# A dynamic convolution with a token-choosing expert layer: softmax sums moved to VectorE in stages, score sums in contiguous reads, x loaded first, a shorter plan for ranks and experts

## The chip, the cores and the metric

The kernel runs on one core of a Trainium2 chip. A core has TensorE (PE, matrix products, weights loaded beforehand), VectorE (DVE), ScalarE (ACT), GpSimd (POOL) and SyncE (SP, which here only issues transfers). Each works through its own queue in order, and semaphores hold an instruction until what it needs is ready. Sixteen DMA engines move data between DRAM and the on-chip memory, SBUF; TensorE writes its products to PSUM, which VectorE and ScalarE read. The metric is the device time of one execution in microseconds.

## The reference, cut to what matters

```python
# x: (8, 4160, 192) float32; weight_gen: (8, 4160, 8 heads, 7 taps)
w = exp(weight_gen - max); w = w / (sum of w over the 7 taps + 1e-9)
conv[b, s, h, :] = sum over k of w[b, s, h, k] * x_pad[b, s + k, h, :]   # 24 channels a head, 6 zeros ahead

scores = einsum('bsd,d->bs', conv, w_gate)
out = conv.copy()
for b in range(8):
    top = indices of the 128 largest scores[b]
    ye = maximum(conv[b, top] @ w1, 0) @ w2        # 192 -> 1024 -> 192
    out[b, top] = conv[b, top] + sigmoid(scores[b, top])[:, None] * ye
```

## The kernel before, in words

**Tiling.** A batch of 4,160 positions is cut into 35 windows of 120; there are 280 windows. x is loaded in fp16 in 20 chunks of 14 windows (`load_x`, L135, issued by GpSimd), a window with its six earlier positions on the 128 partitions; ten chunk buffers exist. The work is in three groups of 2, 3 and 3 batches, that is 70, 105 and 105 windows.

**Softmax of a group.** The windows lie on partitions, the 120 positions in four chunks of 32, 32, 32 and 24 (`WCH`). For each chunk `load_w` (L192) brings the raw weights through SP's queue into one of two buffers. `softmax_a` (L219) takes Exp on ScalarE into the group's buffer `amem` (L227; two such buffers, groups 0 and 2 share one), sums over the seven taps by seven identity matmuls into the PSUM bank `misc` (L235), and takes Ln and Exp(-x) on ScalarE (L241, L243). `softmax_b` (L250) multiplies on VectorE (L257). `wt_head` (L265) transposes one head's weights, eight transposes and a copy; the last one clears a corner on GpSimd (L285).

**Convolution.** A step is four windows; there are 72 steps, and each is also a slot of the plan. `band` (L663) writes, on VectorE, the banded matrices of a step from the transposed weights and a mask; `conv` (L680) runs 32 matmuls of 24 columns with them; `evac` (L723) copies PSUM to SBUF on ScalarE and issues the stores on SP.

**Scores.** The score of a position is the convolution of y = x times the gate per head. `y_unit_a` and `y_unit_b` (L291, L304) transpose x in units of eight blocks, copy on ScalarE and multiply by the gate. For a group whose y is complete, `score_t` (L334) transposes y; `score_p` (L351), once for even and once for odd positions, multiplies weights with shifted y on VectorE and sums over eight heads and seven taps by 56 identity matmuls of 60 columns (L370); `score_s` (L375) copies the sums on ScalarE and sends them to DRAM and back in another layout, issued on SP.

**Selection and experts.** `sel_cand` (L453) takes 24 candidates from each partition, `sel_bcast` (L463) sends them through DRAM to all partitions and prepares values, `sel_rank` (L496) counts ranks on ScalarE and VectorE, `sel_hot` (L510) sorts by one-hot matmuls and `sel_fin` (L527) makes lists and gates. Then per batch `ex_gather` (L598) fetches 128 rows of the result from DRAM, `ex_a`, `ex_h` and `ex_y` (L610, L621, L632) compute the expert, and a scatter writes the rows back.

**Order.** Every engine's queue is written out by hand through a plan: lists of moves per slot. In each slot come `band` of the next step, `conv`, the slot's moves and then `evac` (L896 to L911). Behind step 72 the plan goes on with empty slots that hold only moves.

```python
for si in range(NS):
    if si + 1 < NS:
        band(si + 1)
    conv(si)
    for mv in pre[si] + plan[si]:
        mv()
    evac(si)
```

The softmax of group 1 has a chunk in slots 2, 4, 6 and 8, that of group 2 in slots 27, 29, 31 and 33. The scores begin in slots 13, 33 and 51, candidates are in slot 56, the finished selection in slot 64, and a batch's gather, transposes, hidden layer and output are in slots s, s+2, s+3 and s+4, with s two further for each batch.

## Time and profile before

| | us |
|---|---|
| median of 3 runs | 375.7 |
| lowest and highest | 375.44, 375.74 |
| profiled execution, its own time | 376.66 |
| its span, first to last instruction | 374.9 |

The profile is of one execution. An engine's busy time says how long its instructions ran, not whether anything waited for them; the chain of waits follows the work that ended last back from the end, each step to what released it. Times inside the rows are microseconds from the span's start unless marked ns. PE is a matmul, PEld a weight load, POOLq and SPq an engine's issue of transfers. L with a number is a line of the kernel before. A row of busy time by window has the window, its length, the busy time of PE, PEld, DVE, ACT and POOL with their instructions, the clock granted to TensorE as a share of 2.4 GHz, the busy share of the DMA engines and GB/s.

### The profile page before, as it was taken

To read this page: it belongs to the slowest core of one execution; us is meant where nothing else is said; L and a number is where in the kernel's file an instruction comes from. 1 tells how busy PE (TensorE), PEld (TensorE's weight loads), DVE (VectorE), ACT (ScalarE), POOL (GpSimd) and SP (SyncE) were. 2 spreads that over 40 slices of the span, in tenths; PEclk is the share of its full clock that TensorE was granted. 3 is DMA by queue.
4 is the path that set the end of the run, shared out by engine and by line. 5 is a ranking of instruction groups with operands and counts; after the bars stand their busy time and mean duration, and the time that the engine had idled before them with its cause. 6 is when DMAs were issued, how large, how long until landed. Compare 5 with 4: busy or idle time off the path is not lost.

```text
span 374.9 us, 9170 instructions
## 1 busy us (share of the span) xinstructions
PE 260.0 (69%) x3950; PEld 207.8 (55%) x3950; DVE 205.7 (55%) x197; ACT 181.9 (49%) x300; POOL 59.2 (16%) x110
## 2 busy tenths in 40 slices
PE   0355567778779977477778988887833254999991
PEld 0111465557679867355468977887832143654440
DVE  4322658546743667525455467995499999600000
ACT  1343276656873466556662399763135713332220
POOL 3300393022100111031100100000000003134231
PEclk9999999955885555855655589555555555555555
DMA  8756099999999489989932735464143424340110
GB/s 140 112 107 148 10 197 227 235 214 218 222 210 193 68 178 215 224 230 220 140 81 79 110 75 145 132 172 136 39 131 102 119 75 138 90 123 31 31 33 16
DMA packets 77404, 50.30 MB, mean 134 GB/s; under 512 B 42128, under 2 KB 75792, under 8 KB 77359
## 3 DMA queue, kind: packets, MB, share of 16 engines
q0 software_dynamic: 38256, 16.11, 34.8%
q1 hardware_dynamic: 38655, 33.56, 33.8%
q8 instruction: 32, 0.52, 0.6%
q14 instruction: 13, 0.11, 0.1%
q10 hardware_dynamic: 448, 0.00, 0.1%
HBM read 37.70 MB, written 26.49 MB: 171 GB/s over the span
## 4 chain that ended last, share of the span: by engine, by line
PE 44%; ACT 21%; DVE 15%; DMA 9%; issue 6%; SPq 2%; POOL 1%; ACTq 0%; POOLq 0%; DVEq 0%
PE misc L370 10%; PE misc L235 9%; ACT xT L301 7%; ACT amem L227 5%; DMA out_dram<-co 5%; PE xtps L297 5%; DMA wraw<-in_weight_gen_dram 4%; PE hps L626 4%; PE hps L628 4%; PE cps L704 4%; DVE band__158 L668 3%; PE yeps L636 3%; DVE band__159 L668 3%; ACT co L729 3%; ACT wt L282 2%
## 5 line engine op out<-in xcount | busy, mean ns | idle before, releaser
L668 DVE TENSOR_TENSOR band__158<-wt,mask 128x3840 f16<-128x3840 f16 (+1 forms) x36 | 75.9, 2110 | 21.7 <-PE cps L704 14.9
L668 DVE TENSOR_TENSOR band__159<-wt,mask 128x3840 f16<-128x3840 f16 (+2 forms) x36 | 75.0, 2082 | 10.4 <-PE cps L704 10.3
L729 ACT COPY co<-cps 128x768 f32<-128x768 f32 x70 | 55.9, 802 | 33.3 <-PE cps L704 17.5
L235 PE MATMUL misc<-amem,ident 105*105 105x256 f16 (+3 forms) x84 | 37.7, 602 | 47.4 <-ACT amem L227 47.4
L301 ACT COPY xT<-xtps 128x1024 f16<-128x1024 f16 (+1 forms) x60 | 53.6, 913 | 31.1 <-PE xtps L297 30.4
L235 PEld LDWEIGHTS <-ident 105*105 105x105 f16 (+1 forms) x84 | 14.6, 173 | 65.3 <-issue 59.6
L297 PE MATMUL xtps<-ident,x 128*128 128x128 f16 x420 | 48.5, 291 | 0.0
L704 PE MATMUL cps<-x,band__158 128*128 128x24 f16 x1128 | 36.3, 181 | 16.7 <-DVE band__158 L668 16.4
L704 PEld LDWEIGHTS <-band__158 128*128 128x128 f16 x1128 | 35.9, 105 | 19.9 <-DVE band__158 L668 17.1
L257 DVE TENSOR_TENSOR amem<-amem,r 105x2048 f16<-105x2048 f16 (+3 forms) x12 | 13.9, 1157 | 57.6 <-ACT r L243 57.6
L704 PE MATMUL cps<-x,band__159 128*128 128x24 f16 x1112 | 35.8, 181 | 13.7 <-DVE band__159 L668 10.0
L704 PEld LDWEIGHTS <-band__159 128*128 128x128 f16 x1112 | 35.2, 105 | 17.4 <-DVE band__159 L668 10.5
L370 PE MATMUL misc<-sp,ident 105*105 105x60 f16 (+1 forms) x336 | 37.9, 288 | 5.6 <-DVE sp L360 5.6
L370 PEld LDWEIGHTS <-ident 105*105 105x105 f16 (+1 forms) x336 | 37.4, 177 | 5.7 <-issue 5.7
L297 PEld LDWEIGHTS <-x 128*128 128x128 f16 x420 | 37.6, 132 | 0.0
L156 POOL DMA_DIRECT2D x<-in_x_dram x24 | 25.3, 1073 | 65.6 <-PE cps L704 59.3
L227 ACT ACTIVATE amem<-wraw 105x1792 f16<-105x1792 f32 (+3 forms) x12 | 19.3, 1604 | 13.0 <-DVE rmax L763 10.2
L241 ACT ACTIVATE lnd<-misc 105x256 f32<-105x256 f32 (+3 forms) x12 | 4.4, 368 | 38.7 <-PE misc L235 38.7
L360 DVE TENSOR_TENSOR sp<-amem,Y 105x3840 f16<-105x3840 f16 (+1 forms) x6 | 12.9, 2157 | 17.2 <-PE misc L370 13.5
L274 PE MATMUL wtps<-ident,amem 105*128 105x105 f16 (+1 forms) x192 | 14.8, 235 | 9.3 <-ACT xT L301 5.7
L630 ACT ACTIVATE hT<-hps 128x512 bf16<-128x512 f32 x16 | 9.6, 597 | 23.4 <-PE hps L628 21.8
L626 PE MATMUL hps<-xeT,w_a 128*128 128x128 bf16 x64 | 18.3, 286 | 2.4 <-ACT xeT L616 2.4
(137 smaller groups left out, 302.0 us busy)
## 6 DMA issues: line engine op xcount, KB each, us to landing
out_dram<-co SPq DMA_DIRECT2D x64, 360.0 KB, 4.3
x<-in_x_dram POOLq DMA_DIRECT2D x14, 672.0 KB, 20.2
wraw<-in_weight_gen_dram SPq DMA_DIRECT2D x24, 224.0 KB, 5.8
x<-in_x_dram POOLq DMA_DIRECT2D x8, 336.0 KB, 17.1
wraw<-in_weight_gen_dram SPq DMA_DIRECT2D x8, 168.0 KB, 4.2
x<-in_x_dram POOLq DMA_DIRECT2D x2, 624.0 KB
out_dram<-co SPq DMA_DIRECT2D x5, 180.0 KB, 3.9
out_dram<-co SPq DMA_DIRECT2D x6, 90.0 KB, 3.7
```

Source lines behind the costliest of these rows:

```text
L156: nc.gpsimd.dma_start(out=t[p0:p0 + n, lo - c * CW:hi - c * CW, :], in_=ap_of(x_flat, x_flat.offset + (row0(lo) + off) * D, [[D, n], [W * ...
L227: nc.scalar.activation(out=A[0:n, :, q0:q1, 0:K].rearrange("p c q k -> p q c k"), in_=wr[0:n, 0:nq * M, :].rearrange("p (q m) (h k) -> p q ...
L235: nc.tensor.matmul(out=dv[0:n], lhsT=ident16[0:n, 0:n], rhs=A[0:n, :, q0:q1, k], start=(k == 0), stop=(k == K - 1),)
L274: nc.tensor.transpose(out=tp[:, m, 0:n], in_=am[0:n, o:o + P], identity=ident16[0:n, 0:n])
L297: nc.tensor.transpose(out=tp[:, r - r0, :], in_=xf[:, r * P:(r + 1) * P], identity=ident16[:, :])
L301: nc.scalar.copy(out=xT[:, 0:r1 - r0, :], in_=tp[:, 0:r1 - r0, :])
L370: nc.tensor.matmul(out=sps[0:n, odd], lhsT=ident16[0:n, 0:n], rhs=sp[0:n, :, h, :, k], start=(h == 0 and k == 0), stop=(h == H - 1 and k = ...
L626: nc.tensor.matmul(out=hps[:, t, :], lhsT=w1_a[:, c0:c0 + P], rhs=xeT[:, 0, :], start=True, stop=False)
L628: nc.tensor.matmul(out=hps[:, t, :], lhsT=w1_b[0:64, c0:c0 + P], rhs=xeT[0:64, 1, :], start=False, stop=True)
L668: nc.vector.tensor_tensor(out=bt[:, 0:n * H * BC].rearrange("p (c q m) -> p c q m", q=NQ, m=M), in0=wts[gi][:, l:l + n].rearrange("p w h m ...
L704: nc.tensor.matmul(out=cps[:, w // 2, (w % 2) * D + h * G:(w % 2) * D + (h + 1) * G], lhsT=bt[:, o:o + P], rhs=xwin(g + w)[:, h * G:(h + 1 ...
L729: nc.scalar.copy(out=co[:, 0:n, :].rearrange("p (j w) d -> p j (w d)", w=2), in_=cps[:, 0:n2, 0:2 * D],)
```

## The change: what it does

The branches for a layout that is not used (`HALF`) are gone; this changes no instruction. The rest:

- **Softmax in four stages.** `sm_exp` (ScalarE), `sm_den` (a VectorE sum over the seven taps, in place of the seven matmuls), `sm_r` (Ln and Exp) and `sm_norm` (the multiplication) stand in four slots one after another. Group 1 has a chunk in each of slots 0 to 3, group 2 in slots 23, 25, 27 and 29. Heads are transposed one a slot instead of two.
- **Score sums.** Eight identity matmuls of 480 contiguous columns sum over heads (`score_m`), a slot after the product, and a VectorE sum over the taps reads PSUM; the copy on ScalarE goes. The transfers of scores and of candidates are issued on GpSimd.
- **Start.** Ten x chunks are issued at the start, eight of them before the softmax of group 0 instead of behind it. Only the unused eighth tap of `amem` is cleared, for the first buffer on VectorE, for the second on GpSimd. The four chunks of group 0 are interleaved by stage. The selection's constants move from slot 2 to the start.
- **Order in a slot.** `band` runs two steps ahead with three buffers, `evac` comes right behind `conv`. A unit of y is multiplied behind the next unit's transposes; the last one ends in slot 53 instead of 50 and the scores begin in slots 14, 34 and 53.
- **Selection and experts.** Candidates are in slot 58, the finished selection in slot 63; batches follow each other by one slot, with the four parts in s, s+1, s+2 and s+3, and four buffers for gathered rows.
- **PSUM.** The bank `misc` goes, and its bank becomes a third buffer for transposes, sums and expert outputs.

```diff
-    ps_t = ctx.enter_context(tc.tile_pool(name="ps_t", bufs=2, space=bass.MemoryType.PSUM))
+    ps_t = ctx.enter_context(tc.tile_pool(name="ps_t", bufs=3, space=bass.MemoryType.PSUM))
...
-        den = misc[:, 0:M * H * 4]
-        dv = den[:, 0:M * H * nq].rearrange("p (c q) -> p c q", q=nq)
-        for k in range(K):
-            nc.tensor.matmul(
-                out=dv[0:n], lhsT=ident16[0:n, 0:n], rhs=A[0:n, :, q0:q1, k],
-                start=(k == 0), stop=(k == K - 1),
-            )
-        cq = M * H * nq
-        lnd = smp.tile([P, M * H * 4], FP32, tag="lnd", name="lnd")
-        nc.scalar.activation(out=lnd[0:n, 0:cq], in_=den[0:n, 0:cq], func=AF.Ln)
...
+        n, q0, q1, nq, col, cq = dims(gi, ci)
+        den = smp.tile([P, M * H * 4], FP32, tag="den", name="den")
+        nc.vector.tensor_reduce(
+            out=den[0:n, 0:cq].rearrange("p (c q) -> p c q", q=nq),
+            in_=a_view(gi)[0:n, :, q0:q1, 0:K], axis=AX.X, op=ALU.add,
+        )
...
+    def sm_r(gi, ci):
+        n, q0, q1, nq, col, cq = dims(gi, ci)
+        den = sm[(gi, ci)]
+        nc.scalar.activation(out=den[0:n, 0:cq], in_=den[0:n, 0:cq], func=AF.Ln)
         r2 = smp.tile([P, M * H * 4, 2], FP16, tag="r2", name="r2")
...
+    def score_m(gi, odd):
+        b0, b1 = GROUPS[gi]
+        n = (b1 - b0) * NW
+        sp = sps_.pop((gi, odd))
+        sps = ps_t.tile([P, M // 2, Q, 8], FP32, tag="tps", name="sps")
         for h in range(H):
-            for k in range(K):
-                nc.tensor.matmul(
-                    out=sps[0:n, odd], lhsT=ident16[0:n, 0:n], rhs=sp[0:n, :, h, :, k],
-                    start=(h == 0 and k == 0), stop=(h == H - 1 and k == K - 1),
-                )
+            nc.tensor.matmul(
+                out=sps[0:n].rearrange("p m q k -> p m (q k)"), lhsT=ident16[0:n, 0:n],
+                rhs=sp[0:n, :, h, :], start=(h == 0), stop=(h == H - 1),
+            )
+        if odd == 0:
+            scs[gi] = smp.tile([P, Q, M // 2, 2], FP32, tag="sc", name="sc")
+        nc.vector.tensor_reduce(
+            out=scs[gi][0:n, :, :, odd].rearrange("p q m -> p m q"), in_=sps[0:n, :, :, 0:K],
+            axis=AX.X, op=ALU.add,
+        )
...
+        sc = scs.pop(gi)
+        nc.gpsimd.dma_start(
+            out=sc_d[b0 * NW:b0 * NW + n, :], in_=sc[0:n].rearrange("p q m o -> p (q m o)")
+        )
         for b in range(b0, b1):
-            nc.sync.dma_start(
+            nc.gpsimd.dma_start(
                 out=scores[b * PPB:(b + 1) * PPB, :].rearrange("p (j r) -> p j r", r=BLK),
...
     def sel_bcast():
-        nc.sync.dma_start(out=cand_d[:, :], in_=cv[:, :])
-        nc.sync.dma_start(
+        nc.gpsimd.dma_start(out=cand_d[:, :], in_=cv[:, :])
+        nc.gpsimd.dma_start(
...
+
+    def sel_vals():
...
-    NB = 3 if HALF else 2
+    NB = 3
...
+    XA = 10
     load_w(0, 0)
     load_w(0, 1)
-    load_x(0)
-    make_identity(nc, identity[:])
-    nc.vector.tensor_copy(out=ident16[:, :], in_=identity[:, :])
-    for i in range(2):
-        nc.vector.memset(amem[i][:, :], 0.0)
-    for i in range(NB):
-        nc.vector.memset(bandbuf[i][:, 4 * H * BC:], 0.0)
     nc.vector.memset(emax[:, :], 0.0)
     nc.vector.memset(rmax[:, :], 0.0)
-    nc.vector.memset(ones16[:, :], 1.0)
...
+    nc.vector.memset(a_view(0)[:, :, :, K], 0.0)
+    nc.vector.memset(amem[0][:, M * H * Q * 8:], 0.0)
+    make_identity(nc, identity[:])
+    load_x(0)
+    nc.gpsimd.memset(ones16[:, :], 1.0)
...
+    load_x(1)
...
-    load_x(1)
+    nc.vector.tensor_copy(out=ident16[:, :], in_=identity[:, :])
+    for i in range(NB):
+        nc.vector.memset(bandbuf[i][:, 4 * H * BC:], 0.0)
+    for c in range(2, XA):
+        load_x(c)
...
-    for ci in range(NWC):
-        r2 = softmax_a(0, ci)
-        if ci + 2 < NWC:
-            load_w(0, ci + 2)
-        softmax_b(0, ci, r2)
+    sm_exp(0, 0)
+    load_w(0, 2)
+    sm_exp(0, 1)
+    load_w(0, 3)
+    sm_den(0, 0)
+    sm_den(0, 1)
+    sm_r(0, 0)
+    sm_exp(0, 2)
+    sm_norm(0, 0)
+    sm_den(0, 2)
+    sm_r(0, 1)
+    sm_exp(0, 3)
+    sm_norm(0, 1)
+    sm_den(0, 3)
+    sm_r(0, 2)
+    sm_r(0, 3)
+    sm_norm(0, 2)
+    sm_norm(0, 3)
+    nc.gpsimd.memset(a_view(1)[:, :, :, K], 0.0)
+    nc.gpsimd.memset(amem[1][:, M * H * Q * 8:], 0.0)
+    sel_consts()
     for h in range(H):
         wt_head(0, h, "v" if h % 2 else "s")
-    XA = 10
-    for c in range(2, XA):
-        load_x(c)
...
-    def sm_moves(gi, at, gap):
+        s = k * Y_END // len(seq)
+        at(s, y_unit_a, c, u)
+        if k:
+            at(s, y_unit_b, *seq[k - 1])
+            ydone[seq[k - 1][0]] = s
+    at(s + 1, y_unit_b, *seq[-1])
+    ydone[seq[-1][0]] = s + 1
...
+        if s >= 2:
+            at(s - 2, load_w, gi, 0)
+            at(s - 1, load_w, gi, 1)
         for ci in range(NWC):
-            s = at + ci * gap
-            if ci == 0:
-                plan[max(0, s - 3)].append(lambda: load_w(gi, 0))
-                plan[max(0, s - 3)].append(lambda: load_w(gi, 1))
-            def fa(ci=ci):
-                rr[(gi, ci)] = softmax_a(gi, ci)
-                if ci + 2 < NWC:
-                    load_w(gi, ci + 2)
...
-            plan[s + 1].append(lambda ci=ci: softmax_b(gi, ci, rr.pop((gi, ci))))
-        e = at + NWC * gap + 1
+            t = s + gap * ci
...
         for h in range(H):
-            plan[e + h // 2].append(lambda h=h: wt_head(gi, h, "s"))
-        return e + 4
+            at(t + h, wt_head, gi, h, "s")
+        return t + H
 
     def sc_moves(gi):
-        lastc = (GROUPS[gi][1] * NW - 1) // CW
-        s = ydone[lastc] + 1
-        plan[s].append(lambda: score_t(gi))
-        plan[s + 1].append(lambda: score_p(gi, 0))
-        plan[s + 2].append(lambda: score_p(gi, 1))
-        plan[s + 3].append(lambda: score_s(gi))
+        s = ydone[(GROUPS[gi][1] * NW - 1) // CW] + 1
+        at(s, score_t, gi)
+        at(s + 1, score_p, gi, 0)
+        at(s + 2, score_m, gi, 0)
+        at(s + 2, score_p, gi, 1)
+        at(s + 3, score_m, gi, 1)
+        at(s + 3, score_s, gi)
         return s + 3
...
+    load_w(1, 0)
+    load_w(1, 1)
+    e1 = sm_moves(1, 0, 1)
...
-    e2 = sm_moves(2, max(a0 + 1, first[2] - 18), 2)
-    assert e2 < first[2] - 1
+    e2 = sm_moves(2, max(a0 + 1, first[2] - 22), 2)
...
-    plan[2].append(sel_consts)
-    plan[3].append(load_experts)
+    at(4, load_experts)
     s = s3 + 2
     for r in range(CAND // 8):
-        plan[s].append(lambda r=r: sel_cand(r))
-    plan[s + 1].append(sel_bcast)
+        at(s, sel_cand, r)
+    at(s, sel_bcast)
+    at(s + 1, sel_vals)
     for k in range(ACT_K):
-        plan[s + 3 + k // 4].append(lambda k=k: sel_rank(k))
-        plan[s + 3 + k // 4].append(lambda k=k: sel_rank(ACT_K + k))
+        at(s + 2 + k // 6, sel_rank, k)
...
     for k in range(CAND):
-        plan[s + 6 + k // 12].append(lambda k=k: sel_hot(k))
-    plan[s + 8].append(sel_fin)
-    s = s + 9
+        at(s + 4 + k // 12, sel_hot, k)
+    at(s + 5, sel_fin)
+    s = s + 6
...
     for b in range(B):
-        s0 = max(s, blast[b] + 3)
-        plan[s0].append(lambda b=b: ex_gather(b))
+        s0 = max(s, blast[b] + 2)
+        at(s0, ex_gather, b)
...
-        plan[s0 + 2].append(lambda b=b: ex_a(b))
-        plan[s0 + 3].append(lambda b=b: ex_h(b, 0))
-        plan[s0 + 3].append(lambda b=b: ex_h(b, 1))
-        plan[s0 + 4].append(lambda b=b: ex_y(b))
-        s = s0 + 2
+            at(s0, sel_flag)
+        at(s0 + 1, ex_a, b)
+        at(s0 + 2, ex_h, b, 0)
+        at(s0 + 2, ex_h, b, 1)
+        at(s0 + 3, ex_y, b)
+        s = s0 + 1
...
     band(0)
+    band(1)
...
-        if si + 1 < NS:
-            band(si + 1)
+        if si + 2 < NS:
+            band(si + 2)
         conv(si)
-        for mv in pre[si] + plan[si]:
+        evac(si)
+        for mv in plan[si]:
             mv()
-        evac(si)
```

## Rows read from the trace of the kernel before

**Rows 1.** The page: busy time of the engines, transfers in all.

```profile
PE 260.0 (69%) x3950; PEld 207.8 (55%) x3950; DVE 205.7 (55%) x197; ACT 181.9 (49%) x300; POOL 59.2 (16%) x110
...
DMA packets 77404, 50.30 MB, mean 134 GB/s; under 512 B 42128, under 2 KB 75792, under 8 KB 77359
```

**Rows 2.** Chain of waits up to the first convolution: start, duration, work.

```profile
12.29 1.80 ACT amem L227 x2
...
14.12 3.37 PE misc L235 x7
...
37.06 0.66 PE wtps L274 x8
...
43.44 0.15 POOL wt L285
...
45.83 0.20 PE cps L704
```

**Rows 3.** Chain of waits in the loop: a softmax pair, a score pass.

```profile
63.45 1.80 ACT amem L227 x2
...
73.88 1.80 ACT amem L227 x2
...
109.20 6.14 PE misc L370 x56
```

**Rows 4.** VectorE's instructions in order of time: plain slots, the first candidate.

```profile
238.40 2.16 DVE L668 TENSOR_TENSOR band__159<-wt,mask 128x3840 f16<-128x3840 f16 x1
...
251.98 2.15 DVE L668 TENSOR_TENSOR band__159<-wt,mask 128x3840 f16<-128x3840 f16 x1
...
276.44 0.42 DVE L456 MAX8 cv<-scores 128x8 f32<-128x260 f32 x1
```

**Rows 5.** Busy time by window: selection, experts.

```profile
276.40:311.70 35.30, 12.69 (x310) 10.62 (x311) 34.30 (x85) 13.94 (x35) 0.02 (x1) 0.50 0.39 107
311.70:367.20 55.50, 48.93 (x386) 28.03 (x383) 15.01 (x24) 18.12 (x41) 17.75 (x30) 0.50 0.27 75
```

**Rows 6.** Transfers to landing (median us): weights from 0, weights from 48, gathers.

```profile
wraw<-in_weight_gen_dram SPq DMA_DIRECT2D x12, 224.0 KB, 4.3
...
wraw<-in_weight_gen_dram SPq DMA_DIRECT2D x3, 224.0 KB, 6.8
...
xe__155<-out_dram,sel_i POOLq DMA_INDIRECT x3, 2.7
```

**Rows 7.** Instructions by shape: busy us, mean ns, idle time before them.

```profile
L227 ACT ACTIVATE amem<-wraw 105x1792 f16<-105x1792 f32 x6 | 10.2, 1702 | 2.8 <-DMA wraw<-in_weight_gen_dram 2.8
L257 DVE TENSOR_TENSOR amem<-amem,r 105x2048 f16<-105x2048 f16 x6 | 7.4, 1225 | 30.4 <-ACT r L243 30.4
L243 ACT ACTIVATE r<-lnd 105x512 f16<-105x512 f32 x6 | 3.8, 630 | 0.2
L241 ACT ACTIVATE lnd<-misc 105x256 f32<-105x256 f32 x6 | 2.3, 383 | 20.7 <-PE misc L235 20.7
...
L227 ACT ACTIVATION_READ_ACCUMULATOR amem<-wraw 105x1 f32 x8 | 1.5, 192 | 0.0
...
L456 DVE MAX8 cv<-work 128x8 f32<-128x260 f32 x2 | 0.9, 432 | 0.1
```

**Rows 8.** Chain of waits in the expert stage.

```profile
324.17 1.29 PE yeps L636 x8
...
336.09 1.51 PE yeps L636 x8
342.00 1.51 PE yeps L636 x8
```

**Rows 9.** SP's issues for the last group's scores.

```profile
271.73 0.32 SPq L390 DMA_DIRECT2D sc_d<-sc  x1
273.29 1.28 SPq L394 DMA_DIRECT2D scores<-sc_d  x3
```

**Rows 10.** GpSimd's instructions in order of time.

```profile
66.33 0.57 POOL L591 DMA_DIRECT2D w_b<-in_moe_w_dram  x1 [6.84 <-DMA x<-in_x_dram]
```

More of the change, by code (lines that the diff above doesn't have):

```diff
@@ L24 @@
 HK = H * K
-HALF = False
-W = 112 if HALF else 120
+W = 120
 Q = 15
 M = 8
-BC = 56 if HALF else 120
+BC = 120
 NQ = BC // M
-CW = 16 if HALF else 14
+CW = 14
 CAND = 24
@@ L347, in score_t @@
         yts[gi] = (Y0, Y1)
[L349 removed]
+    sps_ = {}
+    scs = {}
     def score_p(gi, odd):
@@ L360, in score_p @@
         nc.vector.tensor_tensor(
-            out=sp[0:n].rearrange("p m h q k -> p m h (q k)"),
+            out=sp[0:n],
             in0=ap_of(a0, am[0:n, odd * H * Q * 8:odd * H * Q * 8 + 1].offset,
@@ L683, in conv @@
         cps = ps_c.tile([P, 2, 512], FP32, tag="cps", name="cps")
-        if HALF:
-            order = []
-            ws = list(range(n))
-            second = ws[n // 2:] + ws[:n // 2]
-            for wa, wb in zip(ws, second):
-                for h in range(H):
-                    order.append((wa, h, 0))
-                    order.append((wb, h, 1))
-            for w, h, s in order:
-                p0 = 64 * s
+        for w in range(n):
+            for h in range(H):
                 o = (w * H + h) * BC
                 nc.tensor.matmul(
-                    out=cps[p0:p0 + 64, w // 2, (w % 2) * D + h * G:(w % 2) * D + (h + 1) * G],
-                    lhsT=bt[p0:p0 + 64, o:o + 64], rhs=xwin(g + w)[p0:p0 + 64, h * G:(h + 1) * G],
+                    out=cps[:, w // 2, (w % 2) * D + h * G:(w % 2) * D + (h + 1) * G],
+                    lhsT=bt[:, o:o + P], rhs=xwin(g + w)[:, h * G:(h + 1) * G],
                     start=True, stop=True, skip_group_check=True,
                 )
-        else:
-            for w in range(n):
-                for h in range(H):
-                    o = (w * H + h) * BC
-                    nc.tensor.matmul(
-                        out=cps[:, w // 2, (w % 2) * D + h * G:(w % 2) * D + (h + 1) * G],
-                        lhsT=bt[:, o:o + P], rhs=xwin(g + w)[:, h * G:(h + 1) * G],
-                        start=True, stop=True, skip_group_check=True,
-                    )
         cts[si] = cps
@@ L830, in fast_path @@
-    for k, (c, u) in enumerate(seq):
-        plan[ypos[k]].append(lambda c=c, u=u: y_unit_a(c, u))
-        pre[ypos[k] + 1].append(lambda c=c, u=u: y_unit_b(c, u))
-        ydone[c] = ypos[k] + 1
-    first = [next(i for i, s in enumerate(steps) if s[0] == gi) for gi in range(3)]
-    rr = {}
-    def sm_moves(gi, at, gap):
-        for ci in range(NWC):
-            s = at + ci * gap
-            if ci == 0:
-                plan[max(0, s - 3)].append(lambda: load_w(gi, 0))
-                plan[max(0, s - 3)].append(lambda: load_w(gi, 1))
-            def fa(ci=ci):
-                rr[(gi, ci)] = softmax_a(gi, ci)
-                if ci + 2 < NWC:
-                    load_w(gi, ci + 2)
-            plan[s].append(fa)
-            plan[s + 1].append(lambda ci=ci: softmax_b(gi, ci, rr.pop((gi, ci))))
-        e = at + NWC * gap + 1
+    END = NS + 60
@@ new lines, in fast_path, with at @@
+    plan = [[] for _ in range(END)]
+    first = [next(i for i, s in enumerate(steps) if s[0] == gi) for gi in range(3)]
+    def at(s, f, *a):
+        plan[s].append(lambda: f(*a))
+    Y_END = 52
+    seq = [(c, u) for c in range(NCH) for u in range(NU)]
+    ydone = {}
+    for k, (c, u) in enumerate(seq):
+        s = k * Y_END // len(seq)
[4 more added lines that the diff above has]
+    at(s + 1, y_unit_b, *seq[-1])
@@ L908, in fast_path @@
             nextx += 1
-    for si in range(NS, NS + 60):
-        for mv in pre[si] + plan[si]:
+    for si in range(NS, END):
+        for mv in plan[si]:
             mv()
```

129 lines of the change are left out of this document (46 added, 83 removed).

## The prediction

> **What bounds the kernel now.** I read the windows by stage first, then the chain of waits, then the groups of instructions by shape, the DMA queues and the waits of GpSimd's queue. No engine is full over the run: 260 us of TensorE, 206 of VectorE and 182 of ScalarE stand in 374.9 us [rows 1]. What sets the time differs by stage.
>
> Up to the first convolution at 45.8 us one softmax chunk follows another: exp on ScalarE 1.8 us, seven summing matmuls 3.37 us, then Ln and Exp on ScalarE, and only then the next exp [rows 2]. In the loop the same chain stands inside two slots: an exp at 63.45, the next chunk's at 73.88, 10.4 us on [rows 3]. A plain slot is VectorE's band: six slots from 238.40 to 251.98, 2.26 us each [rows 4]. So a chunk adds 10.4 - 4.5 = 5.9 us to its pair of slots. While TensorE waits for the exp and ScalarE for the sums, everything queued behind them on both engines waits too. The score sums (56 matmuls, 6.14 us a pass) stand on the chain as well [rows 3]. From 276 to 312 us VectorE is full with the selection and eight bands (34.3 of 35.3 us), and after that TensorE with the experts (48.9 of 55.5 us), at the lower clock level, 1.2 GHz [rows 5].
>
> **Start.** The change clears only the unused eighth lane of the first buffer on VectorE, so exp no longer waits to 12.29; it waits for weights. A 224 KB transfer lands in 4.3 us in the first 48 us; the second batch's stands third in SP's queue, so I put the first exp at 6. But ten x chunks now load beside the weights, and then the same transfer took 6.8 us [rows 6]. With two weight buffers a chunk is asked for when the exp two chunks before it ends; I charge 6.8 us a chunk, in series: exps at 6.0, 12.8, 19.6 and 26.4. Behind the last come exp, sum, Ln, Exp and multiplication, three quarters of 1.70, 2.0 (below), 0.38, 0.63 and 1.22 plus two accumulator reads of 0.19 [rows 7] and hand-overs: 5.0 us, to 31.4. Eight transposed heads took 6.4 us (37.06 to 43.44 [rows 2]); a third PSUM buffer lets two copies overlap the third's transposes, I take 5.4, to 36.8. GpSimd's clearing and band 0 take 2.4 as before (43.44 to 45.83): first convolution at 39.2, **-6.6 us**. Bounds: 0 (GpSimd late, rival A) and -17 (each fetch at 4.3 us and overlapped, ScalarE's 3.1 us a chunk setting the pace).
>
> **Softmax in the loop**, eight chunks. The seven matmuls go; a VectorE sum over 1,792 fp16 elements comes. No such sum of this size is in the trace. Bounds: the multiplication's pace (1.225 us for 2,048) gives 1.07 us, MAX8's (0.432 us for 260) 2.98 [rows 7]. I take 2.0, the middle of the two, as neither row is nearer in kind. A chunk then costs VectorE 2.0 + 1.22 = 3.2 us and ScalarE 1.70 + 0.19 + 0.38 + 0.63 + 0.19 = 3.1, and in different slots, so that neither waits for the other inside one. It adds 3.2 instead of 5.9: 2.7 less. For group 2 (a chunk each second slot) I take all of it, 4 x 2.7. Group 1 has a chunk in each of its first four slots; chunks 2 and 3 are fetched only when exps 0 and 1 free their buffers, and those slots last about 5.4 us against 6.8 for a transfer; I take off 1 us a chunk: 4 x 1.7. Together **-17.6 us**; with the bounds of the sum -25 to -10. What is late next is VectorE.
>
> The Trainium skill, page "VectorE: DVE Perf Modes", section "Rules for kernel authors", speaks against this edit: it calls tensor_reduce the slowest VectorE operation and advises restructuring away from it. From that page's one element a cycle at 0.96 GHz and some 150 cycles of start-up, 2.03 us is an estimate for 1,792 elements, and the term would be -17.2; no run here shows it yet.
>
> **Score sums**, six passes. 56 matmuls with strided reads become 8 of 480 contiguous columns. The expert output shows contiguous columns at the low level: 8 x 192 in 1.29 us, 0.84 ns each [rows 8], so 3,840 take 3.2 us. A VectorE sum of 420 elements out of PSUM comes behind, 0.25 to 0.70 us by the same two paces; I take 0.6. A pass goes from 6.2 to 3.8, and because sum and next product now stand in one queue I count 2.2 of the 2.4: **-13.2 us**. Bounds: if a column costs what the strided sums do (3.37 us for 1,792, 1.9 ns) 7.2 us a pass, +10 in all; at the upper clock level 1.6 us, -24. The products' reads don't change and the new reads are contiguous, so the first is far off.
>
> **Score transfers on GpSimd's queue.** They leave SP, where stores waited behind them, and stand behind x loads instead. For groups 0 and 1 that is covered: x is loaded up to ten chunks ahead. For group 2 all x is in, and the round trip counts: before, 1.6 us from the first issue to the second, 1.3 for three issues, to the first MAX8 at 276.4, 4.7 us in all [rows 4, 9]. GpSimd took 0.57 us for a small issue [rows 10] and its gathers landed 2.7 us after theirs began [rows 6]: 2.7 + 2 x 0.57 + 2.7 = 6.5 us, **+1.8 us** (0 to +6); two bands run meanwhile, as before.
>
> **Selection, slots.** The last y unit is two slots later and the selection spans six slots instead of nine. But band 65 is the last band ahead of the finished selection in both orders, so VectorE does the same work up to there, and six bands are left for the expert stage in both: 0. The candidates' way through DRAM moves to GpSimd too; the 0.25 us more that an issue takes there (0.57 against 0.32 us [rows 9, 10]) is hidden by the bands and the value preparation that run meanwhile.
>
> **Experts.** An expert takes 5.91 us (336.09 to 342.00) [rows 8], with short waits for the copy of its transposes, the relu and a PSUM buffer. Transposes, hidden layer and output of three different experts now share a slot, with three buffers: I take 0.5 off each, **-4.0 us** (0 to -8). Gathers go one slot ahead, a fourth buffer covers it.
>
> **Evacuation ahead of the slot's other work, bands two ahead, y order:** they remove TensorE's wait for bands; the plain slot is VectorE's band anyway, so 0 (to -6).
>
> **Sum.** -6.6 - 17.6 - 13.2 + 1.8 - 4.0 = -39.6 us. The profiled execution took 376.66 us, 1.0 above the median of the runs (375.7): 337.1 for a profiled one, **336.1** as a median.
>
> **Rivals.**
> A, *the loads get in each other's way*. GpSimd waited 6.84 us for x transfers ahead of an issue of expert weights, which needs no x [rows 10]: its queue holds only so many transfers. Now thirteen x issues go first, and the clearing that band 0 needs is behind them. Weights and stores share the engines with x. Then the start gains nothing (+6.6) and group 1 loses its share (+6.8): 350. Against it: x is then done earlier, and before the loop there are no stores. The Trainium skill, "DMA: Bandwidth & Descriptors", section "Queues, rings and completion order", lets every engine take turns between its queues packet by packet; by that weights are delayed but not starved, which the 4.3 and 6.8 us bear out.
> B, *all waits go and VectorE is full.* It has 206 - 6 (memsets) + 23 (twelve sums) + 4 (six score sums) = 227 us of work. Some 16 of it lie in the start and 16 behind the selection, so 195 between 37 us and the finished selection; at the 97% of the selection stage that takes 201 us, to 238, and with 63 us of experts and end (374.9 - 311.7) the span is 301, the time 302. Halfway there is 319. For it: the plain slots already run so. Against it: score passes still have VectorE wait for TensorE.
> C, *slower: the VectorE sum is dear.* Its place is the eight loop chunks and the four of the start, all then on VectorE's path; 39.6 us over twelve sums is 3.3 us each, so from 5.3 us a sum the gain is gone; at 6 us the time is 384. It needs 3 ns an element against MAX8's 1.6.
> D, *no change*: the waits for sums become waits for transfers of the same length. The 50.3 MB went at 134 GB/s over the span [rows 1]; transfers would have to bind at just that rate, which no row shows.
>
> **Chances.** Forecast 0.69, A 0.15, B 0.09, C 0.05, D 0.02. Measurement here tells 0.2% from no change. All but C and D are faster: 0.93, same 0.02, slower 0.05. The forecast's own range, its terms' bounds put together as independent, is 319 to 349; taking in A and half of B, 316 to 358.
>
> **What would show it.** First convolution near 39 us and weights as the wait before the exps; the loop's exps 7.5 to 8.5 us apart in group 2; VectorE sums of 2 us; score passes of 3.2 us on TensorE; the finished selection near 275; experts 5.4 us apart. Wrong if the first band waits for GpSimd beyond 43 us, if the sum costs over 3 us, if ScalarE sits before exps in group 1 for more than 8 us in all, or if the clock stays up in the expert stage (then 20 us better).

## The result: 333.7 us against 375.7

The changed kernel took 333.68 us as the median of four executions (331.54 to 336.09), the kernel before 375.72: a ratio of 0.887 with a 95% interval of 0.879 to 0.895. On another chip it took 336.23, ratio 0.895 (0.891 to 0.899). The prediction, 336.1, lies between the two. The sum of its terms came out right by luck: the terms did not, as three stages show. Executions of one of these kernels differ by up to 4%, partly with the clock that the expert stage is granted (in the profile of the kernel called start freed below 0.74, that stage taking 48.8 us instead of 57.9 at 0.53), so the stages, read from the profiled execution, stand beside the times. They are cut at the first convolution and at the first MAX8, VectorE's first instruction of the candidates:

| stage, us | before | after | measured | predicted |
|---|---|---|---|---|
| start, to the first convolution | 45.8 | 50.0 | +4.2 | -6.6 |
| loop and last scores, to the first MAX8 | 230.6 | 191.3 | -39.3 | -17.6 - 13.2 + 1.8 = -29.0 |
| selection, experts, end | 98.5 | 93.1 | -5.4 | -4.0 |
| span | 374.9 | 334.4 | -40.5 | -39.6 |

L with a number is from here on a line of the kernel whose row it is. The page of the changed kernel answers to [rows 1]: span, then busy time, share and instructions of each engine.

```profile
span 334.4 us, 8468 instructions
...
PE 187.2 (56%) x3578; PEld 154.8 (46%) x3578; DVE 223.0 (67%) x215; ACT 179.7 (54%) x297; POOL 71.8 (21%) x127
```

TensorE lost 73 us of work and VectorE took on 17. The windows of the changed kernel, answering to [rows 5], are loop with last scores, selection, and experts without the last scatter:

```profile
50.00:241.30 191.30, 127.79 (x2952) 115.39 (x2952) 161.09 (x89) 135.73 (x203) 26.05 (x44) 0.71 0.87 180
241.30:271.20 29.90, 8.15 (x173) 6.58 (x174) 28.32 (x81) 10.96 (x30) 1.36 (x4) 0.50 0.20 54
271.20:329.10 57.90, 47.20 (x396) 29.08 (x392) 15.40 (x24) 18.41 (x41) 21.13 (x31) 0.53 0.26 73
```

In the loop VectorE (third pair of numbers) is busy 161 of 191 us, 84%, and it is the fullest engine there; the selection is still VectorE's (28.3 of 29.9), the experts still TensorE's at the lower clock level (0.53).

**Start.** The chain of waits up to the first convolution, in place of [rows 2]:

```profile
6.50 27.48 DMA x<-in_x_dram
...
34.49 1.08 POOL x L151
...
37.25 4.27 POOL amem L795
...
43.87 0.16 DVE cnum L449
...
46.80 0.75 DVE wt L280
...
47.83 2.17 DVE band__155 L671
...
50.05 1.03 PE cps L690 x32
```

No softmax stands on this chain: it is GpSimd's queue, and the waits of the first 50 us say how (engine and line, what was waited for, us, times, longest):

```profile
POOL x L151 <- DMA x<-in_x_dram: 19.7, 4, 5.5
...
DVE cnum L449 <- POOL pm L448: 16.8, 1, 16.8
ACT amem L225 <- DMA wraw<-in_weight_gen_dram: 12.5, 3, 6.0
```

Four of GpSimd's x issues each wait for an earlier x transfer, so the queue is through with them at 35.6. Behind them stand the gate masks, then a clearing of 960 separate fp16 elements per partition (L795) that takes 4.34 us, then the selection's constants:

```profile
37.18 4.34 POOL L795 MEMSET amem<- 128x960 f16 x1
```

VectorE meanwhile sits 16.8 us at cnum, an instruction of those constants that was put ahead of VectorE's half of the head copies. The band then waits for GpSimd's clearing of a corner (L285, 47.66), which waits for those copies. Group 0's weights were normalised at 27.1; exps ran at 5.7, 13.5, 16.3 and 22.0.

**Loop.** The changed kernel's instructions by shape (busy us, mean ns, idle time before them), answering to [rows 7]:

```profile
L236 DVE TENSOR_REDUCE den<-amem 105x256 f32<-105x1792 f16 x6 | 12.1, 2015 | 7.8 <-ACT amem L225 7.8
...
L376 PE MATMUL sps<-sp,ident 105*105 105x480 f16 x32 | 10.3, 484 | 6.0 <-DVE sp L361 5.9
...
L225 ACT ACTIVATE amem<-wraw 105x1792 f16<-105x1792 f32 x6 | 10.2, 1704 | 6.2 <-DMA wraw<-in_weight_gen_dram 6.2
...
L257 DVE TENSOR_TENSOR amem<-amem,r 105x2048 f16<-105x2048 f16 x6 | 7.3, 1221 | 2.1 <-ACT r L247 2.1
...
L245 ACT ACTIVATE den<-den 105x256 f32<-105x256 f32 x6 | 2.7, 442 | 0.0
```

The sum takes 2.015 us where 2.0 was taken, and the Ln that had 20.7 us of waits ahead of it has none. (The Trainium skill, page "VectorE: DVE Perf Modes", section "Rules for kernel authors", expects tensor_reduce at the slowest mode, and the estimate worked out from that page has the size right; its advice to consider restructuring did not pay here: the kernel before with its sums on VectorE, below, gained 14.2 us.) ScalarE's instructions in order of time show group 2's exps, in place of [rows 3]:

```profile
133.28 1.70 ACT L225 ACTIVATE amem<-wraw 105x1792 f16<-105x1792 f32 x1 [3.56 <-DMA wraw<-in_weight_gen_dram]
...
140.12 1.70 ACT L225 ACTIVATE amem<-wraw 105x1792 f16<-105x1792 f32 x1 [1.09 <-DMA wraw<-in_weight_gen_dram]
...
150.44 1.68 ACT L225 ACTIVATE amem<-wraw 105x1792 f16<-105x1792 f32 x1
...
156.56 1.31 ACT L225 ACTIVATE amem<-wraw 105x1344 f16<-105x1344 f32 x1
```

They are 7.8 us apart on average where 7.5 to 8.5 was said; group 1's, one a slot, stand 4.5 apart (53.8 to 67.3).

The score passes in the same view of TensorE, and the windows of a pass of groups 0, 1 and 2 (granted clock: third number from the end):

```profile
106.21 1.79 PE L376 MATMUL sps<-sp,ident 70*70 70x480 f16 x8
110.75 1.81 PE L376 MATMUL sps<-sp,ident 70*70 70x480 f16 x8 [1.89 <-DVE sp L361]
```

```profile
106.20:108.10 1.90, 1.90 (x26) 1.17 (x23) 1.42 (x2) 1.37 (x2) 0.00 (x0) 1.00 0.80 203
...
178.50:180.40 1.90, 1.82 (x16) 1.19 (x16) 1.33 (x2) 1.90 (x5) 0.00 (x0) 1.00 1.50 197
...
223.70:227.10 3.40, 3.34 (x14) 1.76 (x14) 2.07 (x2) 0.00 (x0) 0.00 (x0) 0.50 0.25 83
```

A pass takes 1.8 us at the upper level, 2.4 GHz, in groups 0 and 1, and 3.4 at the lower in group 2. The old passes took 6.3 us each, and in the trace of before all six stand at 0.50 to 0.57. (The Trainium skill, page "TensorE: Matmul & The Clock Gate", section "Wait — 56ns, not 53.3ns?", gives a stream of matmuls one column per cycle; by an estimate from it eight of 480 columns take 3.2 us or 1.6, a little under both rows.)

**Last scores.** VectorE's and GpSimd's instructions in order of time, in place of [rows 4, 9]:

```profile
233.27 0.60 DVE L382 TENSOR_REDUCE sc<-sps 105x60 f32<-105x420 f32 x1 [1.38 <-PE sps L376]
...
235.84 2.15 DVE L671 TENSOR_TENSOR band__155<-wt,mask 128x3840 f16<-128x3840 f16 x1
241.25 0.43 DVE L457 MAX8 cv<-scores 128x8 f32<-128x260 f32 x1 [3.26 <-DMA scores<-sc_d]
```

```profile
234.16 0.57 POOL L391 DMA_DIRECT2D sc_d<-sc  x1 [28.55 <-DVE sc L382]
236.31 0.58 POOL L395 DMA_DIRECT2D scores<-sc_d  x1 [1.59 <-DMA sc_d<-sc]
237.17 1.11 POOL L395 DMA_DIRECT2D scores<-sc_d  x2 [0.28 <-issue]
```

From the end of the last sum (233.87) to MAX8 7.4 us pass, against 4.7 before, and VectorE runs out of bands and waits 3.26.

**Experts.** From the finished selection (271.2) to the end 63.2 us pass, as before. The output matmuls of the first seven experts are 4.8 to 6.2 us apart, 5.5 on average (281.9 to 314.8), in place of the 5.9 of [rows 8]; the eighth comes 11.0 us behind. TensorE's wait there:

```profile
PE xeTp L616 <- DMA xe__154<-out_dram,sel_i: 4.9, 1, 4.9
```

GpSimd's instructions in order of time show the last gather (L604) behind the scatter of batch 6 (L647), which itself waits for VectorE's last step of that batch:

```profile
317.06 0.98 POOL L647 DMA_INDIRECT out_dram<-ye,sel_i  x1 [3.84 <-DVE ye L642]
...
318.35 1.05 POOL L604 DMA_INDIRECT xe__154<-out_dram,sel_i  x1 [0.23 <-issue]
```

### The profile page after: what moved, and what is told of

Same layout as the page of the kernel before. It is cut to its first block, busy times and chain, and to the rows that moved or that the text cites. A ratio compares the mean times of both kernels' runs of the same rounds, so it can differ in the third digit from the quotient of the medians.

```text
span 334.4 us, 8468 instructions
## 1 busy us (share of the span) xinstructions
PE 187.2 (56%) x3578; PEld 154.8 (46%) x3578; DVE 223.0 (67%) x215; ACT 179.7 (54%) x297; POOL 71.8 (21%) x127
## 4 chain that ended last, share of the span: by engine, by line
issue 36%; DMA 30%; PE 10%; POOL 9%; ACT 7%; DVE 4%; SPq 2%; POOLq 1%; ACTq 0%
DMA out_dram<-co 11%; DMA wraw<-in_weight_gen_dram 9%; DMA x<-in_x_dram 8%; ACT xT L301 2%; PE cps L690 2%; PE sps L376 2%; ACT co L715 2%; SPq L207 2%; PE wtps L274 1%; PE xtps L297 1%; DVE sp L361 1%; POOL x L151 1%; POOL amem L795 1%; ACT amem L225 1%; POOL out_dram L647 1%
## 5 line engine op out<-in xcount | busy, mean ns | idle before, releaser
L671 DVE TENSOR_TENSOR band__155<-wt,mask 128x3840 f16<-128x3840 f16 x24 | 51.6, 2149 | 2.5 <-POOL wt L285 2.5
L671 DVE TENSOR_TENSOR band__156<-wt,mask 128x3840 f16<-128x3840 f16 x24 | 51.6, 2150 | 0.0
L671 DVE TENSOR_TENSOR band__157<-wt,mask 128x3840 f16<-128x3840 f16 (+2 forms) x24 | 47.6, 1983 | 4.8 <-PE cps L690 4.8
L297 PE MATMUL xtps<-ident,x 128*128 128x128 f16 x420 | 43.6, 263 | 0.5 <-issue 0.4
L274 PE MATMUL wtps<-ident,amem 105*128 105x105 f16 (+1 forms) x192 | 14.9, 246 | 42.7 <-DVE amem L257 27.1
L151 POOL DMA_DIRECT2D x<-in_x_dram x24 | 25.4, 1066 | 43.4 <-PE cps L690 22.2
L236 DVE TENSOR_REDUCE den<-amem 105x256 f32<-105x1792 f16 (+3 forms) x12 | 22.8, 1898 | 17.5 <-ACT amem L225 17.5
L297 PEld LDWEIGHTS <-x 128*128 128x128 f16 x420 | 32.2, 117 | 0.8 <-issue 0.7
L274 PEld LDWEIGHTS <-amem 105*128 105x128 f16 (+1 forms) x192 | 12.1, 122 | 42.8 <-DVE amem L257 27.1
L315 PE MATMUL yps<-gmat,xT 128*128 128x8 f16 x140 | 16.5, 169 | 25.6 <-ACT y L324 25.3
L690 PEld LDWEIGHTS <-band__156 128*128 128x128 f16 x768 | 22.3, 101 | 10.6 <-DVE band__156 L671 10.2
L282 ACT COPY wt<-wtps 128x840 f16<-128x840 f16 (+1 forms) x20 | 16.8, 841 | 18.8 <-PE wtps L274 18.6
L690 PEld LDWEIGHTS <-band__155 128*128 128x128 f16 x768 | 22.9, 101 | 6.0 <-DVE band__155 L671 5.1
L321 PE MATMUL yps<-gmat,xT 128*128 128x8 f16 x140 | 16.7, 170 | 15.7 <-ACT xT L301 15.7
L315 PEld LDWEIGHTS <-xT 128*128 128x128 f16 x140 | 13.2, 104 | 26.5 <-ACT xT L301 26.3
L690 PEld LDWEIGHTS <-band__157 128*128 128x128 f16 x704 | 21.3, 102 | 7.1 <-DVE band__157 L671 6.2
```

The lines of the kernel that those rows point to most:

```text
L151: nc.gpsimd.dma_start(out=t[p0:p0 + n, lo - c * CW:hi - c * CW, :], in_=ap_of(x_flat, x_flat.offset + (row0(lo) + off) * D, [[D, n], [W * ...
L236: nc.vector.tensor_reduce(out=den[0:n, 0:cq].rearrange("p (c q) -> p c q", q=nq), in_=a_view(gi)[0:n, :, q0:q1, 0:K], axis=AX.X, op=ALU.add,)
L274: nc.tensor.transpose(out=tp[:, m, 0:n], in_=am[0:n, o:o + P], identity=ident16[0:n, 0:n])
L282: nc.scalar.copy(out=dst, in_=src)
L297: nc.tensor.transpose(out=tp[:, r - r0, :], in_=xf[:, r * P:(r + 1) * P], identity=ident16[:, :])
L315: nc.tensor.matmul(out=yps[:, 2 * q, :], lhsT=lhs, rhs=gmat[:, 0, :], start=True, stop=False, skip_group_check=True)
```

## Experiments

The table has the first convolution, the stretch from there to MAX8, and that from MAX8 to the end, us, each from one profile. Where an edit leaves the loop all but as it is (the changed kernel twice, start freed, constants later, gather early), it still lay between 189.2 and 193.3, so a difference in the loop holds to about 2 us. For three kernels no ratio is on record; they are read by their stages.

| kernel | median | ratio to before (95%) | start | loop | rest |
|---|---|---|---|---|---|
| before | 375.7 | 1 | 45.8 | 230.6 | 98.5 |
| changed | 333.7 | 0.887 (0.879 to 0.895) | 50.0 | 191.3 | 93.1 |
| changed, other chip | 336.2 | 0.895 (0.891 to 0.899) | 50.7 | 191.1 | 93.1 |
| start freed | 321.6 | 0.856 (0.848 to 0.864) | 34.5 | 193.3 | 85.4 |
| constants later only | 328.8 | 0.868 (0.863 to 0.874) | 45.1 | 193.0 | 93.4 |
| x late | 328.6 | 0.873 (0.867 to 0.879) | 33.6 | 201.9 | 91.7 |
| staged, sums on TensorE | 338.0 | 0.902 (0.895 to 0.909) | 44.7 | 197.0 | 93.3 |
| before, sums on VectorE | 361.7 | 0.963 (0.957 to 0.969) | 40.9 | 220.5 | 98.5 |
| strided score sums | 354.4 | 0.945 (0.938 to 0.952) | 45.3 | 215.6 | 91.7 |
| old slot order | 336.4 | none | 50.5 | 191.3 | 93.2 |
| gather early | 329.7 | none | 50.8 | 189.2 | 88.4 |
| scores on SP | 327.6 | none | 46.0 | 190.4 | 94.0 |
| combined | 321.4 | 0.855 (0.851 to 0.860) | 39.9 | 190.0 | 89.3 |
| more output buffers | 314.1 | 0.837 (0.832 to 0.841) | 39.9 | 184.0 | 88.7 |

**The changed kernel again**, on the chip that also ran constants later only, combined and more output buffers.

> The changed kernel once more, unedited, so that the others stand beside it on one chip. Both theories: 331 to 336. In the other profiles with an unedited start the first convolution stood between 44.7 and 50.8 us; the theory that its place is set by how soon x transfers land expects it in that stretch again, the theory that it is fixed expects 50.

The first convolution stood at 50.7 with 20.3 us of x waits, which both theories allow. Over the seven profiles with the unedited order of the start it stood at 50.0 to 50.8 where GpSimd's x waits were 19.7 to 20.4 us (four of them), and at 44.7 to 46.0 where they were 14.4 to 15.7 (three): x transfers set it. Why they land sooner in some executions no run shows.

**The start freed.**

```diff
+    nc.vector.memset(a_view(1)[:, :, :, K], 0.0)          # beside amem[0]'s
+    nc.vector.memset(amem[1][:, M * H * Q * 8:], 0.0)
...
-    nc.gpsimd.memset(a_view(1)[:, :, :, K], 0.0)
-    nc.gpsimd.memset(amem[1][:, M * H * Q * 8:], 0.0)
-    sel_consts()
...
+    at(2, sel_consts)
```

> Theory (the start is lost to GpSimd's queue and to what stands behind it): the selection's constants go back to slot 2 and the second buffer's eighth lane is cleared by VectorE (0.9 us) instead of GpSimd (4.34 us). The heads' copies on VectorE then no longer stand behind an instruction that waits for a GpSimd constant, and GpSimd reaches the clearing that band 0 needs right behind its last mask, at 37 to 38 us. First convolution at 40 instead of 50.0, and the time falls by about as much: 322 to 327 against 333.7. Rival 1 (the waits for x transfers alone set it): first convolution stays at 48 to 50, time 332 to 335. Rival 2 (the gain of the start is lost in the first slots, where group 1's chunks follow one another in each slot): first convolution at 40, but the convolution of slot 10 is as late as in the changed kernel, time 331 to 335.

First convolution at 34.5, further than expected, and the loop only 2 us longer: the gain of the start is kept. (The 7.7 us that its profile gains behind MAX8 come with the higher clock there.) The chain of waits of this kernel:

```profile
27.26 3.98 PE wtps L274 x64
31.27 0.75 DVE wt L280
...
32.13 0.15 POOL wt L285
32.30 2.17 DVE band__155 L671
...
34.52 1.03 PE cps L690 x32
```

Heads follow the softmax at once, and eight of them take 4.0 us of TensorE. x waits were short here (13.9 us); the combined kernel below, with the same start, had 20.0 us of them and its first convolution at 39.9.

**Constants later only**, the half without the two clearings.

> Half of the experiment with the free start: only the selection's constants go back to slot 2; GpSimd still clears the second buffer's eighth lane. Theory (the larger part is the VectorE instruction that waits for a constant of GpSimd ahead of the heads' copies): heads done by 34 us, and band 0 then waits for GpSimd alone, which reaches its clearing at about 42 us behind the 4.34 us memset: first convolution at 41 to 44, time 324 to 330. Rival (the slow memset and the x waits are the larger part): first convolution at 45 to 48, time 329 to 334.

The first convolution, 45.1, lies in the rival's stretch, the time, 328.8 us, in the theory's: neither half is clearly the larger. The chain of this kernel names the remainder:

```profile
38.51 4.27 POOL amem L795
...
42.79 0.05 POOL wt L285
...
42.87 2.17 DVE band__155 L671
...
45.08 0.92 PE cps L690 x28
```

So with near-equal x waits (20.3, 21.0, 20.0 us) the constants as a whole, GpSimd's own 3 us of them and VectorE's wait, cost 5.6 us of the start (50.7 to 45.1), the slow clearing 5.2 (45.1 to 39.9, the combined kernel below).

**x late.**

```diff
-    for c in range(2, XA):
-        load_x(c)
     gsel = ...
...
     for h in range(H):
         wt_head(0, h, "v" if h % 2 else "s")
+    for c in range(2, XA):
+        load_x(c)
```

> The changed kernel with x chunks 2 to 9 asked for behind group 0's heads, as in the kernel before; all else stays. Theory (x first costs the start): GpSimd has its masks, constants and clearing done before the heads, nothing on VectorE waits for them; first convolution at 34 to 38 instead of 50.0, and since x chunk 2 is first wanted in slot 7, little of it is lost: 320 to 328. Rival (x first pays, or only moves the wait): the x issues then stand in GpSimd's queue between the clearings of the bands' weights and group 1 meets them; what the start gains the first twenty slots lose, 332 to 338.

First convolution at 33.6, and 328.6 us, just beyond the theory's stretch, since the loop pays 10.6 us for it (201.9 against 191.3), much of what the start gains, as the rival had it; the transfers that the start no longer makes are made there (busy share of the DMA engines 1.03 instead of 0.87). Against the start freed, where x does go first, the loop is 8.6 longer and the start the same: x first is worth some 8 us of the loop if nothing urgent stands behind it.

**Staged, sums on TensorE**; and **before, sums on VectorE**.

```diff
-        nc.vector.tensor_reduce(out=den..., in_=a_view(gi)[0:n, :, q0:q1, 0:K], ...)
+        den = ps_t.tile([P, M * H * 4], FP32, tag="tps", name="denp")
+        for k in range(K):
+            nc.tensor.matmul(out=dv[0:n], lhsT=ident16[0:n, 0:n], rhs=a_view(gi)[0:n, :, q0:q1, k], ...)
```

> The changed kernel with its stages, but the seven summing matmuls into a PSUM tile in place of VectorE's sum. Theory (the stages pay, the engine of the sum hardly matters): TensorE takes 12 x 3.4 us more and VectorE 12 x 2.0 us less, neither waits for the other inside a slot; 328 to 339. Rival 1 (VectorE's sum itself is what pays): each sum is back on the way at 3.4 instead of 2.0 us and the PSUM buffers are held longer: 12 x 1.4 to 12 x 3.4 more, 350 to 374. Rival 2 (VectorE is the bound of the loop): its 24 us less come out in full for the eight chunks of the loop, 316 to 321.

The second has the opposite edit in the kernel before, with exp, sum, Ln and Exp still in one slot.

> The kernel before with one edit, the seven summing matmuls replaced by VectorE's sum; exp, sum, Ln and Exp still stand in one slot. Theory (the stages pay): the sum is 2.0 instead of 3.4 us but stands behind a band in VectorE's queue, and VectorE has 24 us more to do; 370 to 382 against 375.7. Rival (the sum's engine pays): 1.4 us and the hand-over are saved on each of twelve chunks, 352 to 362.

The first fits its theory: loop 5.7 us longer, time 338.0. The second fell: its rival had 352 to 362, and 361.7 came, 14.2 us less than the kernel before on the same chip (375.9) from the sum's engine alone; in the profiles 4.9 in the start and 10.1 in the loop. Windows of the two loops, staged first:

```profile
44.70:241.70 197.00, 149.58 (x3008) 125.83 (x3008) 148.06 (x81) 136.48 (x203) 26.05 (x44) 0.78 0.90 182
```

```profile
40.90:261.40 220.50, 158.10 (x3144) 149.84 (x3144) 153.54 (x81) 135.37 (x202) 32.38 (x56) 0.60 0.93 172
```

With stages, 22 us of TensorE work (149.6 against 127.8) replace 13 of VectorE's and cost 5.7: the work is mostly hidden. Without stages the sum's length and hand-over are paid each time, about 1.3 us in the start and in the loop (an exp each 4.9 us instead of 6.2, and 8.9 instead of 10.2 us). What the stages are worth by themselves is not shown: no run takes them back with the rest unchanged.

**Strided score sums.**

```diff
-            nc.tensor.matmul(out=sps[0:n].rearrange(...), lhsT=ident16[0:n, 0:n],
-                rhs=sp[0:n, :, h, :], start=(h == 0), stop=(h == H - 1))
+            for k in range(K):
+                nc.tensor.matmul(out=sps[0:n], lhsT=ident16[0:n, 0:n], rhs=spv[0:n, :, h, :, k],
+                    start=(h == 0 and k == 0), stop=(h == H - 1 and k == K - 1))
...
-        nc.vector.tensor_reduce(out=scs[gi]..., in_=sps[0:n, :, :, 0:K], axis=AX.X, op=ALU.add)
+        nc.scalar.copy(out=scs[gi]..., in_=sps[0:n])
```

> The changed kernel with the old score sums: 56 matmuls of 60 strided columns a pass and ScalarE's copy in place of 8 of 480 contiguous columns and VectorE's sum. Theory (a pass lies on the way of the slots and of the end of the scores): TensorE takes 6.1 instead of 1.7 to 3.4 us a pass, VectorE 0.6 less; six passes, 2.5 to 3.5 us each: 348 to 355. Rival (in groups 0 and 1 VectorE hides it, so only the two last passes count): 338 to 341.

354.4, as the theory had it: the loop is 24.3 us longer. Up to the last group's score transposes that is 17.4, or 4.35 for each of four passes, near the 6.3 less 1.8 of the rows; the last group pays 6.9. Whether the stride, the short length or the weight load ahead of each of the 56 counts for most is not separated; in the old passes weight loads (the second pair of numbers) are busy throughout, in the new one of group 2 for 1.76 of 3.40 us. All six stand at 0.50 to 0.64 again; two of them in this kernel's windows:

```profile
112.70:119.00 6.30, 6.26 (x61) 6.26 (x61) 4.12 (x2) 0.00 (x0) 0.00 (x0) 0.50 0.03 10
182.60:188.90 6.30, 6.29 (x62) 6.29 (x62) 1.25 (x1) 2.48 (x4) 0.00 (x0) 0.64 1.01 190
```

**Old slot order.**

```diff
-    NB = 3
+    NB = 2
...
-        if si + 2 < NS:
-            band(si + 2)
+        if si + 1 < NS:
+            band(si + 1)
         conv(si)
-        evac(si)
         for mv in plan[si]:
             mv()
+        evac(si)
```

> The changed kernel with the old order in the loop: evacuation last in a slot, one band ahead, two band buffers. Theory: a plain slot goes back from 2.05 to about 2.26 us because VectorE waits for the convolution's end at each slot; over some 50 slots +6 to +10: 340 to 344. Rival (the order gave nothing, as the prediction had it): 331 to 336.

The rival held, which was the prediction's own view: the loop is 191.3 in both, and ten plain slots take 21.6 us against 21.5. What brought a plain slot from 2.26 us to 2.15 was therefore not the order. Bands that wait for nothing stand 2.07 us apart in both kernels; the stretch read at 2.26 held two waits for a convolution, of 0.70 and 0.19 us.

**Gather early.**

```diff
-        s0 = max(s, blast[b] + 2)
+        s0 = max(s, blast[b] + 1)
```

> The changed kernel with the last batch's gather one slot earlier, ahead of batch 6's scatter in GpSimd's queue. Theory: TensorE's wait of 4.9 us for the last expert's rows goes; 4 to 5 us less in the profile, 328 to 330. Rival (the last expert's rows wait for something else, or its slots move together and wait for the weights of another stage): 333 to 335.

TensorE's 4.9 us wait is gone. The windows of selection and experts of this kernel, the latter 52.9 instead of 57.9 us at the same clock:

```profile
240.00:270.00 30.00, 8.31 (x179) 6.73 (x180) 28.39 (x82) 11.13 (x30) 1.55 (x4) 0.50 0.20 53
270.00:322.90 52.90, 47.01 (x389) 28.88 (x386) 15.27 (x24) 18.34 (x40) 20.96 (x31) 0.53 0.29 79
```

**Scores on SP**: the score and candidate transfers back from nc.gpsimd to nc.sync.

> The changed kernel with the score and candidate transfers on SP's queue, as before. Theory (SP issues and lands them quicker): from the end of the last score sum to the first MAX8 4.7 instead of 7.4 us, time 330 to 332. Rival (the queue behind the stores costs as much): 7 us or more again, 333 to 337.

From the last sum's end (232.02) to MAX8 4.4 us passed instead of 7.4, in VectorE's instructions in order of time:

```profile
231.42 0.60 DVE L382 TENSOR_REDUCE sc<-sps 105x60 f32<-105x420 f32 x1 [1.38 <-PE sps L376]
...
236.42 0.43 DVE L457 MAX8 cv<-scores 128x8 f32<-128x260 f32 x1 [0.27 <-DMA scores<-sc_d]
```

So the 3 us of the round trip are shown, but not that they reach the end: the loop, 190.4, is only 0.9 shorter, within its spread, and what this profile gains on the changed kernel's is otherwise its start at 46.0, where x landed sooner. The median, 327.6, is lower than this explains.

**Combined** (start freed, gather early, scores on SP), and **more output buffers** on top of it:

```diff
-    cop = ctx.enter_context(tc.tile_pool(name="cop", bufs=3))
+    cop = ctx.enter_context(tc.tile_pool(name="cop", bufs=5))
-    NB = 3
+    NB = 2
...
-        if si + 2 < NS:
-            band(si + 2)
+        if si + 1 < NS:
+            band(si + 1)
```

> The three edits that gained together: selection's constants in slot 2 and the lane cleared by VectorE, the last gather a slot earlier, scores and candidates on SP's queue. Theory (they lie in different stages, start, end of the scores, last expert, and add up): -12 to -15, -3 and -5 from 333: 311 to 315. Rival (the stages that follow take some back, as transfers fill the loop): 317 to 322, that is no better than the free start alone.

> The combined kernel with five output buffers instead of three, paid for by two band buffers instead of three (bands one ahead). Theory A (ScalarE's evacuations wait for stores to free a buffer, 15 to 20 us over the first forty slots, and that sets their 3.2 to 3.3 us a slot): the first thirty slots gain 5 to 10 us, time 303 to 309. Theory B (the transfers themselves fill that stretch, the engines of the DMA being busy 0.9 to 1.4 of it): more buffers only let more stores wait in the queues, 311 to 317.

Combined: 321.4, 14.8 less than the changed kernel on the same chip, but in the rival's stretch and not the theory's 311 to 315, which counted from 333; nor is it better than the 321.6 of the start freed, which was taken on another chip with shorter x waits. In stages start -10.8, loop -1.1, rest -3.8 against the changed kernel there, for the -12 to -15, -3 and -5 that the theory had for start, end of the scores and last expert. With five output buffers the loop falls from 190.0 to 184.0 and the time to 314.1, in the stretch of theory B. Yet not as B had it: the buffers did shorten the loop (two band buffers instead of three do not: the old slot order, which has two, leaves it as it was). ScalarE's waits in the combined kernel, then TensorE's in the other, both from 40 to 190 us:

```profile
ACT co L715 <- DMA out_dram<-co: 14.5, 9, 3.6
```

```profile
PE cps L690 <- DVE band__155 L671: 25.0, 11, 8.5
```

The wait for stores is gone altogether, and TensorE waits for bands instead, of which only two are held; theory A named the right wait and overrated it. This version is 16% below the kernel before and 6.5% below the changed one (0.8365 / 0.8948).

## Why the prediction came out right, and where its steps did not

**Start: wrong sign.** The step that failed was the first convolution at 39.2 us "with GpSimd's clearing and band 0 taking 2.4 as before". Weights came sooner than charged (last exp at 22.0, predicted 26.4), but GpSimd was not free, and the prediction's own sign of being wrong came: band 0 waits for GpSimd to 47.8, not 43. Rival A's mechanism, which had 0.15, held for the start; its other half, that group 1 loses its share, did not, ScalarE waiting 1.6 us for weights there. A put the gain at nothing; two things that no term held turned it into a loss, the selection's constants, with an instruction of them ahead of VectorE's copies (5.6 us), and the slow clearing (5.2 us). Both show in the diff: the clearing and the constants are added between the x issues and the heads. The prediction counted the clearing of buffer 0, on VectorE, and did not walk GpSimd's queue for that of the second buffer or for the constants.

**Softmax in the loop: the pace came, the size is not shown.** -17.6 was predicted. The loop's -39.3 less 24.3 for the score sums and +2.7 for the round trip leaves -17.7, but that agreement shows nothing: the remainder also holds x first, which the prediction gave no term in the loop and which is worth 8.6 to 10.6 us there, and the cost of three more bands, below. Less x first, 7 to 9 us are left for softmax and all else, to about 2 us. What the rows show of the term itself: a sum of 2.015 us, exps of group 2 7.8 us apart where the kernel before has 10.2, which is 2.4 a chunk for the 2.7 charged, and of group 1 4.5. In the start freed and x late, group 2's stand 9.4 and 11.2 apart, so the pace is not set by the softmax alone. Rival C is out with 2.0 us a sum.

**Score sums: mis-sized,** -13.2 for what measured -24.3. The price of 3.2 us a pass was read from the expert stage's rows at the lower clock; it held in group 2 (3.36) and in groups 0 and 1 the pass ran at the upper level in 1.8. So four passes gained 17.4 us instead of 8.8, the last two 6.9 instead of 4.4. The text had a bound of -24 for all six at the upper level; that -24.3 came with four of six is chance.

**Score transfers:** +1.8 predicted, +2.7 measured for the round trip; putting them back takes 3.0 off it.

**Experts: right inside, lost at the end.** The 0.5 us taken off each expert came (5.5 apart; 5.4 was said), but the stage stayed at 63.2 us, since the last gather now stood behind batch 6's scatter in GpSimd's queue and cost 4.9 us. "Gathers go one slot ahead, a fourth buffer covers it" is the step that failed: the queue, not the buffer, held the gather.

**Selection: a shift.** The last y unit does end two slots later (slot 52; the 53 ahead of the prediction is one too many). As said, 66 bands run ahead of the finished selection in both traces. But 61 instead of 58 of them now run before MAX8, where VectorE has waits to fill, so that the stage that VectorE fills holds five instead of eight and takes 29.9 us instead of 35.3; it ends at 271.2 where 275 was said. That is the 5.4 us of the rest; what the three bands cost the loop is not shown.

**Order: nothing,** as said. Rival B's full VectorE was not reached: 84% in the loop, with stores, weights and bands waiting in turn. D is out.

So an over-rated start and expert stage (10.8 and 4.0 us) and a dearer round trip (0.9) were offset by under-rated score sums (11.1) and a shorter selection (5.4), and in the loop x first, which had no term, seems to fill what softmax fell short. The total was met by luck.

## What to carry to other kernels

When issues that can block are moved to the front of a queue, list everything behind them on that engine, and on the engines that wait for it; here a group of small constants, with one 0.16 us instruction that waited for them, cost 5.6 us. Eight wide matmuls of contiguous columns took 3.4 us where 56 short strided ones took 6.3, both at a granted clock of 0.50, and in four of six passes the wide ones ran at the upper level and took 1.8. Splitting a dependent chain over slots and making its slowest link shorter are not additive: the shorter sum was worth 10 us of the loop without the stages and under 6 with them. A remainder that equals a forecast term shows nothing until what else it holds has been measured; here it held x first.
